# Second dense layer three tiles behind the first, first MoE products in two groups, and a new instruction order

## The chip, the core and the metric

The kernel runs on one core of a Trainium2 chip. The engines are TensorE (PE in the profile; PEld is its weight load), VectorE (DVE), ScalarE (ACT), GpSimd (POOL) and SyncE (SP), which here only issues DMAs. The metric is the device time of one execution in microseconds (us); the median of three runs is compared.

## What is computed

Three stages follow each other: attention in which a query sees only keys of its own hash bucket, a dense mixture of four experts, and a dense block with SoLU and layer norm. The sizes are 2 batches x 768 rows = 1536 tokens, 8 heads of 64, width 512, hidden width 1024.

```python
# attention, per batch and head (768 x 64)
mask = bucket(q @ proj)[:, None] == bucket(k @ proj)[None, :]   # 6 sign bits each
attn = softmax(where(mask, q @ k.T / 8, -1e9)); x = attn @ v
# MoE: every token through all 4 experts
out = sum(p[:, e] * (relu(x @ w1[e]) @ w2[e]) for e in range(4))
# dense block
h = out @ w_in; solu = h * softmax(h)
ln = (solu - mean) / sqrt(var + 1e-6) * g_ln
return ln @ w_out
```

All results have float32 accuracy. The kernel gets it by splitting each operand into a high and a low half (in the 32-bit format that TensorE takes at full rate, or in f16) and adding three products: high x high, high x low, low x high.

## The kernel before

**Staging.** The 12 tiles of 128 tokens form 4 chunks of three. Attention of the first chunk (`attn_first`) runs alone; attention of chunks 1 to 3 is spread over the MoE of chunks 0 to 2; then comes the dense block (`dense`) over all 12 tiles.

**The first chunk's attention.** Keys and queries of the first two heads (`ln` and `y` serve as their buffers) are split, turned by TensorE, projected with `lhs_w` for the sign bits; the other six heads go in pairs (`project_pairs`). For head h, `unit(h)` issues the DMAs that bring operands of its scores from on-chip tiles into two alternating buffers: `kC` (here named wsa_104), `qC` (wsb_106), `kB` and `qB`. Even heads use kB_125 and qB_127, odd heads kB_126 and qB_128. Scores of 128 queries are four matmuls (wsa x wsb and kB x qB, twice); DVE takes the row maximum, ACT the exponential into a `p` tile, TensorE turns p in six 128x128 transposes (`idn,p`), ACT or DVE copies them out, and 6 or 12 matmuls with v follow (`t,hl` for the first four heads, `t,vs` or `xh,vs` later). `av_out` divides, and after every second head splits the result into one quarter (one of KD = 4 slices of 128) of `xh` and `xl`, the operands of the MoE's first products. Between these stand the loads of v for a maximum (`ln<-in_v_dram`, twice 768 KB), of the domain probabilities (`dp`), and of the first expert weights (`wra`, `wrb`).

**The MoE.** `moe_a(c, s)` makes hidden slice s of chunk c: 12 matmuls over the four quarters of xh and xl into one PSUM bank. `split_h` evicts it with ACT (relu, high half) and DVE (low half). `moe_b` multiplies by w2. Weights are split into halves on ACT, POOL and DVE (`wsa`, `wsb` from `wra`, `wrb`).

**The dense block.** `first(i)` makes tile i's hidden row block (24 matmuls of 512 columns in four groups), then a chain of small steps on DVE and ACT (`ln_tiles`), then the high and low halves in f16 (`copy_by`, `sub_by`) and two DMA transposes. `second(i)` makes 24 matmuls of 512 columns in eight groups from them. Program order is first(i), then second(i - lag).

**What sets the order.** Every operation is recorded with its dependencies (`Recorder`), a matmul group as one operation. `emit` then issues them in the order of the table `ORDER`: each number is the place, among the operations still left, of the next one. `FORMS` names the engine of each operation that several can do (A is ACT, V is DVE, G is POOL), `BANKS` its PSUM bank. Each engine works through its own queue in that order. All operations are issued from line 389, so the profile shows that line for all; the tiles tell them apart.

## Time and profile before

| | us |
|---|---|
| median of three runs | 850.31 |
| the three runs | 849.22, 853.28, 850.31 |
| the profiled execution | 850.63 |
| its span, from the first to the last instruction | 848.8 |
| TensorE busy within the span | 827.0 |
| VectorE busy | 673.3 |
| ScalarE busy | 456.1 |
| GpSimd busy | 262.6 |

The span leaves out 1.8 us of the profiled execution. A timeline row gives start, duration, engine, operation and how many were merged; in brackets stands the idle time of the engine ahead of it and what ended it. A matmul's duration has its way through the array in it, so successive ones overlap: three matmuls of 512 columns show 0.81 us and six show 1.46.

### The profile page before, as it was taken

To read this page: it belongs to the slowest core of one execution; us is meant where nothing else is said; L and a number is where in the kernel's file an instruction comes from. 1 tells how busy PE (TensorE), PEld (TensorE's weight loads), DVE (VectorE), ACT (ScalarE), POOL (GpSimd) and SP (SyncE) were. 2 spreads that over 40 slices of the span, in tenths; PEclk is the share of its full clock that TensorE was granted. 3 is DMA by queue.
4 is the path that set the end of the run, shared out by engine and by line. 5 is a ranking of instruction groups with operands and counts; after the bars stand their busy time and mean duration, and the time that the engine had idled before them with its cause. 6 is when DMAs were issued, how large, how long until landed. Compare 5 with 4: busy or idle time off the path is not lost.

```text
span 848.8 us, 13127 instructions
## 1 busy us (share of the span) xinstructions
PE 827.0 (97%) x4431; PEld 529.4 (62%) x4431; DVE 673.3 (79%) x1425; ACT 456.1 (54%) x846; POOL 262.6 (31%) x296
## 2 busy tenths in 40 slices
PE   6898999999999999999999999999999999999998
PEld 5666898888988555656555555555555554444443
DVE  7779868788878999988577898853477989998782
ACT  5658747797874476674325566432145444444331
POOL 2125543466732132343213214241033332210130
PEclk9999999999999999999999999999999999999999
DMA  8787776999999999999756999825249766245352
GB/s 204 204 222 193 203 251 160 264 254 265 271 261 298 293 281 263 266 224 226 165 156 171 245 231 244 215 63 125 75 131 231 258 212 197 79 108 119 81 105 93
DMA packets 241747, 167.83 MB, mean 198 GB/s; under 512 B 167824, under 2 KB 213008, under 8 KB 241680
## 3 DMA queue, kind: packets, MB, share of 16 engines
q1 hardware_dynamic: 241680, 167.00, 75.6%
q8 instruction: 35, 0.57, 0.3%
q14 instruction: 32, 0.26, 0.1%
HBM read 103.51 MB, written 19.73 MB: 145 GB/s over the span
## 4 chain that ended last, share of the span: by engine, by line
PE 79%; DVE 9%; DMA 4%; issue 3%; POOL 3%; ACT 1%; SPq 1%; DVEq 0%; POOLq 0%; ACTq 0%
PE PS L389 79%; DVE ln L389 3%; POOL ln L389 1%; DMA wsb<-wsb 1%; DVE sm L389 1%; SPq L389 1%; DMA ln<-in_moe_w_out_dram 1%; DMA winD<-ln 1%; DMA kD<-stk 1%; DVE tmp L389 1%; DMA ln<-in_moe_w_in_dram 1%; POOL p L389 1%; DVE wsa1h L389 0%; DVE p L389 0%; DMA ln<-in_k_dram 0%
## 5 line engine op out<-in xcount | busy, mean ns | idle before, releaser
L389 ACT ACTIVATE p<-PS,sm 128x768 f32<-128x768 f32 x96 | 95.0, 990 | 39.5 <-POOL sm L389 18.2
L389 DVE TENSOR_REDUCE sm<-PS 128x1 f32<-128x768 f32 x96 | 90.9, 950 | 15.0 <-PE PS L389 13.8
L389 POOL TENSOR_SCALAR sm<-sm 128x1 f32<-128x1 f32 x93 | 33.8, 364 | 152.2 <-DVE sm L389 102.0
L389 PE MATMUL PS<-xh,wsa 128*128 128x384 f32 x256 | 69.7, 337 | 0.0
L389 PE MATMUL PS<-kB,qB 80*128 80x384 f32 x192 | 65.2, 339 | 0.5 <-DMA kB<-vs 0.5
L389 PEld LDWEIGHTS <-hha0h 128*128 128x128 f16 x400 | 37.4, 98 | 40.7 <-issue 3.7
L389 ACT ACTIVATE hha0h<-PS 128x384 f16<-128x384 f32 (+1 forms) x66 | 31.8, 487 | 56.2 <-PE PS L389 56.0
L389 POOL TENSOR_SCALAR ln<-ln 128x512 int32<-128x512 int32 x26 | 36.1, 1388 | 82.1 <-DVE ln L389 69.9
L389 PEld LDWEIGHTS <-wsa1h 128*128 128x128 f16 x408 | 39.6, 98 | 28.7 <-issue 0.6
L389 PE MATMUL PS<-kC,qC 128*128 128x384 f32 x144 | 56.3, 391 | 1.3 <-DVE hxa L389 1.3
L389 PEld LDWEIGHTS <-wsa0h 128*128 128x128 f16 x408 | 39.3, 98 | 28.4 <-issue 1.1
L389 DVE SCALAR_TENSOR_TENSOR hl<-p,sm,hl 128x768 f16<-128x768 f32 x48 | 49.7, 1039 | 8.6 <-POOL hl L389 4.7
L389 PE MATMUL PS<-xh1h,ln 128*128 128x384 f16 x192 | 50.5, 327 | 0.0
L389 DVE SCALAR_TENSOR_TENSOR hxa0h<-PS,hha0h 128x384 f16<-128x384 f32 x64 | 35.0, 550 | 19.2 <-ACT hha0h L389 19.1
L389 PE MATMUL PS<-wsb0h,hha0h 128*128 128x512 f16 x164 | 48.9, 380 | 0.2 <-DVE fit L389 0.2
L389 PEld LDWEIGHTS PS<-xh,wsa 128*128 128x128 f32 x256 | 46.7, 188 | 0.5
L389 PEld LDWEIGHTS <-ln 128*128 128x128 f16 x336 | 32.1, 98 | 22.9 <-issue 1.3
L389 PE MATMUL PS<-wsb1h,hha0h 128*128 128x512 f16 x152 | 45.3, 380 | 0.0
L389 PE MATMUL PS<-xl,wsa 128*128 128x384 f32 x128 | 42.9, 335 | 0.0
L389 PE MATMUL PS<-xh1h,wsa0h 128*128 128x384 f16 x160 | 42.4, 327 | 0.0
L389 PE MATMUL PS<-xh1h,wsa1h 128*128 128x384 f16 x160 | 42.0, 326 | 0.0
L389 PE MATMUL PS<-wsb,hha 128*128 128x512 f32 x132 | 41.9, 398 | 0.0
(331 smaller groups left out, 2262.6 us busy)
## 6 DMA issues: line engine op xcount, KB each, us to landing
wra<-in_moe_w_dram SPq DMA_DIRECT2D x52, 512.0 KB, 5.0
wrb<-in_moe_w_dram SPq DMA_DIRECT2D x52, 512.0 KB, 5.0
kC<-kD SPq DMA_DIRECT2D x24, 384.0 KB, 4.5
kB<-kD SPq DMA_DIRECT2D x24, 240.0 KB, 4.2
vr<-in_v_dram SPq DMA_DIRECT2D x28, 192.0 KB, 4.0
qD<-stk SPq DMA_DIRECT2D x27, 192.0 KB, 3.4
qC<-qD SPq DMA_DIRECT2D x24, 192.0 KB, 3.9
ln<-in_moe_w_in_dram SPq DMA_DIRECT2D x8, 512.0 KB, 4.4
```

The source lines that it names most:

```text
L389: fn(**{key: self.now(x) for key, x in kw.items()})
```

## The change

The program gets the same matmuls, 4399 of them with the same columns in total, and the same 573 DMA issues and branches on SP. Three things differ.

In `moe_a` the first three hidden slices of chunk 0 are recorded as two groups: nine matmuls over the first three quarters, and three over the last. In `dense` the lag is 3. The f16 halves of a tile and their transposes no longer share one of three tiles: the transposes go round four half tiles, the halves alternate between two (both in the tile t320h).

```diff
-        with rec.group():
-            for kk in range(KD):
-                for w, x in ((wh, xh), (wh, xl), (wl, xh)):
+        for part in (range(0, KD - 1), range(KD - 1, KD)) if c == 0 and s < 3 else (range(KD),):
+            with rec.group():
+                for kk in part:
+                    for w, x in ((wh, xh), (wh, xl), (wl, xh)):
...
+        halves = [t.rearrange("p a r q -> p (a r q)")[:, j * 2 * FF2:(j + 1) * 2 * FF2] for t in t16_r.t for j in range(2)]
...
-                x = t16_r.t[i % 3].rearrange("p a r q -> p (a r q)")
-                x16, y16 = x[:, 0:2 * FF2], x[:, 2 * FF2:4 * FF2].rearrange("p (a k q) -> p a k q", a=2, q=128)
+                x16 = halves[4 + i % 2]
+                y16 = halves[i % 4].rearrange("p (a k q) -> p a k q", a=2, q=128)
...
-        lag = 2
+        lag = 3
```

The tables `ORDER`, `FORMS` and `BANKS` are new throughout; of `FORMS` the first line:

```diff
-AVAAVVAVVVAAAAVAAAVAAVVAVAAAAGVAVAVGVAGVAVAVAVAAVGGGAAVAGVAVGAVAVGGVGVGVAGVVVVAAVGVGVVVAGVVAVVAGAAVAVGGVAGAGV
+VGAVAAVAVAAVAAVVAVAAAAVAVAAAVAGVAGGAVVGVGAAVGAVAAVVGAAVAAVVVGAAVVVAVAAAVVVGAGVGGAGGAAAVVAVVAVAAVVGVVVGGVAAAGAG
```

They move operations between engines: DVE has 1369 instructions for 1409, ACT 689 for 686, POOL 338 for 301.

On SP, at the place where the operands of head 2 are sent for (wsa_104 from wsa_105, wsb_106, kB_125, qB_127), the order before was:

```order
L389 DMA wsa_104<-wsa_105 64x768 x2
L389 DMA qB_127<-wsb_106 64x384
L389 DMA dp<-in_moe_domain_probs_dram 128x2x24
L389 DMA kB_125<-wsa_105 64x768
L389 DMA ln_113<-in_v_dram 128x4x384
L389 DMA kB_125<-vs_76 16x768
L389 DMA wsb_106<-wsb_106 64x384 x2
L389 DMA qB_127<-kC_68 16x384
```

The same place now, from the first operand of head 2 on:

```order
L389 DMA wsa_104<-wsa_105 64x768
L389 DMA kB_125<-wsa_105 64x768
L389 DMA ln_113<-in_v_dram 128x4x384
L389 DMA wsb_106<-wsb_106 64x384
L389 DMA wsa_104<-wsa_105 64x768
L389 DMA qB_127<-wsb_106 64x384
L389 DMA vr_73<-in_v_dram 128x384
L389 DMA kB_125<-vs_76 16x768
L389 DMA wsb_106<-wsb_106 64x384
L389 DMA qB_127<-kC_68 16x384
L389 DMA ln_113<-in_v_dram 128x4x384
```

The load of `dp` has left (it now stands among the operands of heads 4 and 5), the first 768 KB load, which stood ahead of the place before, is now third, and the second comes behind the last operand of head 2.

On PE, before the first MoE product (xh_93 x wsa_104), the order before was this, with `t_84,vs_75` the last head's product with v:

```order
L389 MATMUL PS<-idn,p_79 128x128 x6
L389 MATMUL PS<-idr,hl_65 128x128 x3
L389 MATMUL PS<-idr,hl_64 128x128 x3
L389 MATMUL PS<-t_84,vs_75 128x384 x12
L389 MATMUL PS<-stk_67,lhs_w 128x384
L389 MATMUL PS<-idr,hl_65 128x128 x3
L389 MATMUL PS<-idr,hl_64 128x128 x3
L389 MATMUL PS<-stk_66,lhs_w 128x384
L389 MATMUL PS<-stk_67,lhs_w 128x384
L389 MATMUL PS<-stk_66,lhs_w 128x384
L389 MATMUL PS<-xh_93,wsa_104 128x384
```

Now two of the nine-matmul groups begin ahead of head 6's product with v (`xh_94,vs_74`); their end and what follows reads:

```order
L389 MATMUL PS<-xl_95,wsa_104 128x384
L389 MATMUL PS<-xh_93,wsa_104 128x384 x2
L389 MATMUL PS<-xl_95,wsa_104 128x384
L389 MATMUL PS<-xh_93,wsa_104 128x384
L389 MATMUL PS<-idn,p_77 128x128 x2
L389 MATMUL PS<-idn,p_78 128x128 x4
L389 MATMUL PS<-idn,p_77 128x128 x4
L389 MATMUL PS<-xh_94,vs_74 128x384 x4
L389 MATMUL PS<-hha_108,vs_74 128x384 x2
```

So 18 matmuls of the MoE moved ahead of the last two heads' products; the third group of nine stands right behind the last head's.

On POOL, at the end of the dense block, the order before was this; TENSOR_TENSOR with ln_113 makes a tile's low half, TENSOR_SCALAR from ln_113 its high half:

```order
L389 TENSOR_TENSOR t_82<-ln_113,t_82 128x1024
L389 TENSOR_SCALAR wsb1h<-wrb_103,fit 128x1024
L389 TENSOR_TENSOR t_82<-ln_113,t_82 128x1024
L389 TENSOR_SCALAR t_83<-ln_113 128x1024
L389 TENSOR_SCALAR t320h<-ln_113 128x1024
L389 TENSOR_TENSOR t320h<-ln_113,t320h 128x1024
L389 TENSOR_SCALAR t_82<-ln_113 128x1024
L389 TENSOR_TENSOR t_83<-ln_113,t_83 128x1024
```

And now:

```order
L389 TENSOR_SCALAR wsb0h<-wrb_102,fit 128x1024
L389 TENSOR_SCALAR hl_81<-y_112,ys 128x512
L389 TENSOR_TENSOR t320h<-ln_113,t320h 128x1024
L389 TENSOR_SCALAR wsb1h<-wrb_103,fit 128x1024
L389 TENSOR_SCALAR wsb0h<-wrb_102,fit 128x1024
L389 TENSOR_TENSOR t320h<-ln_113,t320h 128x1024
L389 TENSOR_SCALAR t320h<-ln_113 128x1024
L389 TENSOR_TENSOR t320h<-ln_113,t320h 128x1024 x3
L389 TENSOR_SCALAR t320h<-ln_113 128x1024
L389 TENSOR_TENSOR t320h<-ln_113,t320h 128x1024 x3
```

POOL makes eight of the eleven low halves in place of four, and two high halves in place of three.

## Rows read from the trace of the kernel before

**Rows 1.** The page: busy time by engine; the chain that ended last.

```profile
PE 827.0 (97%) x4431; PEld 529.4 (62%) x4431; DVE 673.3 (79%) x1425; ACT 456.1 (54%) x846; POOL 262.6 (31%) x296
...
PE 79%; DVE 9%; DMA 4%; issue 3%; POOL 3%; ACT 1%; SPq 1%; DVEq 0%; POOLq 0%; ACTq 0%
```

**Rows 2.** Stretches: length, busy PE, PEld, DVE, ACT, POOL, granted clock, DMA, GB/s.

```profile
33.00:60.00 27.00, 26.39 (x130) 20.29 (x131) 21.53 (x43) 14.66 (x31) 3.10 (x11) 0.94 0.77 201
60.00:80.00 20.00, 16.22 (x93) 13.27 (x92) 17.88 (x39) 15.56 (x39) 9.87 (x18) 1.00 0.79 198
80.00:95.00 15.00, 13.25 (x85) 11.10 (x84) 13.34 (x33) 12.90 (x30) 11.20 (x16) 1.00 0.59 159
...
300.00:636.00 336.00, 336.00 (x1860) 193.46 (x1859) 255.27 (x477) 167.97 (x316) 93.41 (x119) 1.00 0.79 192
...
735.00:849.00 114.00, 110.02 (x514) 50.24 (x512) 85.33 (x312) 41.59 (x63) 13.88 (x9) 1.00 0.42 95
```

**Rows 3.** Timeline of PE around the first scores of head 2.

```profile
33.08 0.66 PE L389 MATMUL PS<-wsa,wsb 128*128 128x384 f32 x1 [2.26 <-DMA wsb<-wsb]
...
36.43 0.43 PE L389 MATMUL PS<-wsa,wsb 128*128 128x384 f32 x1
```

**Rows 4.** Timeline of SP, the issues between head 0's and head 2's scores.

```profile
20.92 1.11 SPq L389 DMA_DIRECT2D wsa<-wsa  x2
...
22.71 1.35 SPq L389 DMA_DIRECT2D dp<-in_moe_domain_probs_dram  x1
...
25.12 0.59 SPq L389 DMA_DIRECT2D ln<-in_v_dram  x1
...
28.37 0.56 SPq L389 DMA_DIRECT2D qB<-kC  x1
```

**Rows 5.** The chain of waits from 0 to 76 us: start, us, what.

```profile
26.38 6.28 DMA wsb<-wsb
```

**Rows 6.** The start: SP's third issue, and DVE's wait for the key load.

```profile
1.64 1.88 SPq L389 DMA_DIRECT2D ln<-in_k_dram  x3
...
5.08 0.36 DVE L389 CAST t<-ln 128x384 fp32r<-128x384 f32 x1 [0.90 <-DMA ln<-in_k_dram]
```

**Rows 7.** Groups by form on DVE and POOL, 0 to 97 us: count, busy, mean ns.

```profile
L389 DVE COPY t<-PS 128x512 f32<-128x512 f32 x5 | 3.4, 685 | 0.2 <-ACT p L389 0.2
...
L389 DVE TENSOR_TENSOR t<-ln,t 128x384 fp32r<-128x384 f32 x2 | 1.1, 559 | 0.7 <-ACT t L389 0.7
...
L389 POOL TENSOR_SCALAR p<-p,sm 128x768 f32<-128x768 f32 x9 | 8.2, 917 | 1.7 <-DVE sm L389 1.5 <-ACT hha L389 0.2
```

**Rows 8.** Timeline of PE, the end of the first chunk's attention.

```profile
82.86 0.63 PE L389 MATMUL PS<-idn,p 128*128 128x128 f32 x4 [0.24 <-DVE xp L389]
83.97 0.88 PE L389 MATMUL PS<-idn,p 128*128 128x128 f32 x6 [0.48 <-POOL p L389]
...
90.76 2.36 PE L389 MATMUL PS<-t,vs 128*128 128x384 f32 x12 [0.55 <-DVE t L389]
```

**Rows 9.** Timelines of POOL, DVE and PE from 143 to 148 us.

```profile
143.99 2.53 POOL L389 TENSOR_TENSOR wsa<-wra,wsa 128x1024 fp32r<-128x1024 f32 x1 [5.09 <-ACT wsa L389]
...
144.20 2.36 DVE L389 TENSOR_SCALAR big<-big 128x2 f32<-128x2 f32 x1
...
147.07 0.45 PE L389 MATMUL PS<-kC,qC 128*128 128x384 f32 x1 [1.27 <-DVE hxa L389]
```

**Rows 10.** The dense block: SP and PE timelines, then DVE's and POOL's low halves.

```profile
743.83 4.12 SPq L389 DMA_TRANSPOSE t<-t  x2
...
750.74 1.46 PE L389 MATMUL PS<-wsb0h,t 128*128 128x512 f16 x6
...
796.71 0.81 PE L389 MATMUL PS<-wsb1h,t 128*128 128x512 f16 x3
...
L389 DVE TENSOR_TENSOR t<-ln,t 128x1024 f16<-128x1024 f32 x5 | 6.1, 1225 | 0.2 <-ACT t L389 0.2
...
L389 POOL TENSOR_TENSOR t<-ln,t 128x1024 f16<-128x1024 f32 x3 | 6.4, 2133 | 57.9 <-ACT t L389 51.5 <-DVE st L389 6.4
```

More of the change, by code (lines that the diff above doesn't have):

```diff
@@ new lines @@
+GGGAGAAAGVAGGAGGVVGAAGAVAGAAAGAGAVGVGVGGVGVGAAGVVVAGAGAAAGGAGVAVAAGVAGAAGGAVAAAAGGGAAVVAVVGVAAAGGAGAVVAVGVVVVA
+GVAAGAAGVAAVVGVGGAAAAGGVAVVGAGVVAVAGVAAAVVGVVAGVGVAAAGVVAVAGGGAVAGGAGAGVGGAGAVVGVVAGVGVAAVAGGAAGGAAVAGGGVGAAAV
+GGAGGAGAAAVVAGVVGAVVAAVGGGVVAGAVAGVVVVAGVGAAGAGAAGGAGAAAVAAAVVGAAGVAVAAGGGAAVVGVAVVGVAGVGAVAVGVAVAVAVVVGAAGAAV
+AGAVVVAVAVAVVAGAGVAAVAVVVGAVAVGGGVGVVAGGGAAGAVAGAAGAVGAVAAGAVAAAAVVAVAAAAVVGAGGGAGAAAGAGAGGAVAGAAGGAAAGAVAVAVA
+VVGVAAGGAAAVAVGAAVGAAAVAAGAAGAVGAAAGGVAGVVAAAGAGGAAVGVVGVAVVGVAGVAAGVVAGGGVGAGAGVAGGVAAGGVVVGGGGAAGVAAVVGVAAAG
@@ L136 @@
+AVVAGAGGVGGAVAAAGGVGAVVGAVGAGVAGGGVGVVGGAAAVAAVVAGAVAVAAGGGAVAGGVVVAVAVAAVAGGVGAAGGGVGVGVGAGAGGVAGAGGVGAAGAAGG
+VGAVAAAAGGAVGGVAVGGGAGGGAGAAGGVGGGVGGVGGGGVGAAGGAGAAVVVGGVVVVAVGGVVGGGGAVGVGAVGGGGGGVVGGAVVVVGVVVAGVAGVAGVAGAG
+AVAGGAAVGAAAVAVVVAVAAGAVAAVAAAVAAVAVAAGAAVAGAVGGAGAAGGAGGGAGGVVAAVAVAGAVAGVGAGVGAGVGVAAVAVA
 """
 BANKS = """
-13574057136701352170350134163560241306013421602354163571074153102604213601320654315360321560143025406756171076
-10572676573654361205326356357474636353615024362364363634535735436546024613767376766736737637363563467656015725
@@ L141 @@
-76744364634363420163463564763573653164023164653436353436341062341543636743467337447642163045435463461304216436
-45364356633062134614653636436457453012561525763513071236471201203156347625013477346574623105642006436243062146
-054537402
+30653171607534023742503720145641403601342076364201305640206310341643216043061045230413460132453412041276120177
+01273537454641320634365736536535653463140326143246346334634673661430216343676763673636736737363767354567041627
+56764635436341620163456336545643654632051746563436353573756132401361634676437634764701253466434757361026343463
@@ L144 @@
+56343645463052631035743537655316423452072564307350646702153603540314347637204120420640610521642060436243631046
+740246060
 """
@@ L1348, in moe_a @@
         n = 0
-        with rec.group():
-            for kk in range(KD):
-                for w, x in ((wh, xh), (wh, xl), (wl, xh)):
-                    T.matmul(
-                        out=ps[:, 0:N],
-                        lhsT=w[:, kk, j * 128:(j + 1) * 128],
-                        rhs=x[:, kk, 0:N],
-                        start=(n == 0),
-                        stop=(n == 3 * KD - 1),
-                    )
-                    n += 1
+        for part in (range(0, KD - 1), range(KD - 1, KD)) if c == 0 and s < 3 else (range(KD),):
+            with rec.group():
+                for kk in part:
+                    for w, x in ((wh, xh), (wh, xl), (wl, xh)):
+                        T.matmul(
+                            out=ps[:, 0:N],
+                            lhsT=w[:, kk, j * 128:(j + 1) * 128],
+                            rhs=x[:, kk, 0:N],
+                            start=(n == 0),
+                            stop=(n == 3 * KD - 1),
+                        )
+                        n += 1
         hT["m", c, s] = split_h(ps, N, True, c == 0)
```

9 lines of the change are left out of this document (removed), and 200 rows, old and new, of the table ORDER.

## The prediction

> **What bounds the kernel now.** I read the busy times first: TensorE (PE) works 827.0 of the 848.8 us of the span, and the chain that ended last lies on PE for 79% [rows 1]. The stretches then say where the other 22 us lie. From 300 to 636 us PE is busy 336.00 of 336.00 at a granted clock of 1.00, and the dense block is much the same: 110.02 of 114.00, with the last store in it [rows 2]. The change leaves the matmuls and their columns alone, so in the middle there is nothing to win; a new order can only open holes there. The holes that are there lie in the first 100 us, in the first chunk's attention: 16.22 busy of 20.00 from 60 to 80 us and 13.25 of 15.00 from 80 to 95, 5.53 idle together [rows 2].
>
> The causes differ by place. At 33.08 PE has waited 2.26 us for a transfer into wsb, an operand of head 2's scores [rows 3]; from 33 to 60 us the granted clock is 0.94 on average [rows 2], since behind that wait the clock is at the lower of its two levels (1.2 of 2.4 GHz) for a while: the first score matmul takes 0.66 us, where one of the same shape takes 0.43 at 36.43 [rows 3]. From 60 to 95 us DVE is the fullest of the helpers, 17.88 + 13.34 = 31.2 of 35 us busy [rows 2], and PE's brackets name DVE and POOL [rows 8].
>
> The sum goes against the profiled execution, 850.63 us, of which 848.8 is the span and 1.8 lies outside; I leave the 1.8 as it is. The median of the runs, 850.31, is 0.3 below it, so I use one scale for both.
>
> **The change part by part.**
>
> *A, the start.* SP's third row issues three key loads in 1.88 us, 0.63 each, and DVE then waits 0.90 us for the load of head 1's keys [rows 6]. In the new order that load is second and no longer third, up to 0.63 sooner, and the cast would start that much sooner. Against it, one low half of these first keys goes from DVE to POOL. No row has this shape on POOL; in the dense block the same kind costs 2133 ns there against 1225 on DVE [rows 10], a factor of 1.74, so the 559 ns of DVE [rows 7] would become 0.97, 0.41 more. Range -0.9 (the whole wait) to +0.41; I take **-0.5**, nearer to the issue, since other low halves stay on DVE.
>
> *B, head 2's operands.* The chain shows the transfer into wsb from 26.38 us on, 6.28 us long [rows 5], though it is a small on-chip copy. Ahead of it stand two loads of v, 768 KB each; the second was issued at 25.12 [rows 4]. At the 201 GB/s of the stretch behind it [rows 2] one such load is 786,432 bytes / 201 = 3.9 us of the DMA engines. SP itself takes from 20.92 to 28.93 (28.37 + 0.56) for this list, 8.0 us without a pause, 1.35 of them for dp [rows 4]. The new order takes dp out and puts the second 768 KB load behind the last operand; ten issues are left which at about 0.6 us make some 6.4 us, 1.6 sooner. A DMA queue 3.9 us shorter and an issue 1.6 us sooner are against a wait of 2.26, so the wait should go, and with it the half clock, 27.00 x 0.06 = 1.62 us. Together 3.88 at most. The first big load still stands third in the list, and the queries' copies behind it; I take **-3.0**, range -3.88 to 0.
>
> *C, relief of DVE.* Up to the first MoE eviction DVE has eight instructions fewer by the order: four evictions of 128x512 (685 ns each, 2.74 us) and four smaller ones net, each between 0 and 0.559 [rows 7], so 2.7 to 5.0 us. POOL gets rid of four of its nine p<-p,sm at 917 ns, 3.7 us [rows 7]; ACT takes over part of both, and has room: 15.56 of 20 and 12.90 of 15 [rows 2]. What of it reaches PE is bounded by PE's idle time there, 5.53 less D's 1.27, so 4.26. DVE is full to 31.2 of 35, so part of the relief only lengthens its own pauses. I take about half the bound, **-2.0**, range -4.26 to 0. The price if ACT becomes late is the rival of the moved wait, below.
>
> *D, groups of nine.* The three bubbles before 82.86, 83.97 and 90.76 make 0.24 + 0.48 + 0.55 = 1.27 us [rows 8]. Two groups of nine now stand ahead of head 6's product with v. Twelve matmuls of 384 columns take 2.36 us [rows 8], so the 18 bring 3.5 us of work for a time in which PE waits for p to be copied. The third group of nine stands behind the last head's product and covers the way of that head's last quarter into xh. The quarter-wise split of xh and xl was there already, so the groups need no new operand. But only bubbles behind the point where they stand can be filled; I take **-0.8**, range -1.27 to 0.
>
> *E, POOL and DVE side by side.* At 143.99 a POOL instruction of two inputs takes 2.53 us, and at 144.20 a DVE instruction on 128x2 elements takes 2.36 [rows 9]; the two end together (146.52 and 146.56). PE then waits 1.27 for what DVE does next [rows 9]. So one can hold the other up. POOL has 37 instructions more, among them nine more with two inputs of 768 or 1024 elements (30 before). One of the 30 cost PE 1.27. By that rate the nine cost 0.4, and I take **+0.5**. Ends: the place at 147 us goes in the new order, -1.27, or three of the nine fall as badly, +3.8.
>
> *F, the dense block.* A product of 512 columns costs (1.46 - 0.81) / 3 = 0.217 us [rows 10]. The lag is counted in program order; the table decides where the products stand. Between the end of a tile's first layer and its first second-layer product stand, by the order, 133 products before and 124 now for tile 0, 1 to 4 within 9 of before, 122 and 200 for tile 10, 176 and 95 for tile 11; behind the last tile's first layer, up to that tile's own turning by PE, 162 and 72. So the room for tile 0 shrinks by 9 x 0.217 = 1.95 us. In the trace its transposes are issued until 747.95 (743.83 + 4.12) and its first product starts at 750.74 [rows 10]: 2.79 us for the landing, and PE loses nothing. How much of it is slack, no row says. The new t16 halves free the buffers sooner and DVE has fewer steps ahead. For the last tile 72 x 0.217 = 15.6 us are left for its chain. Low halves on POOL are 2133 - 1225 = 0.91 us later [rows 10]. Where the products cover, all of this is free; I take **+0.2**, range 0 to 1.95.
>
> Sum: -0.5 - 3.0 - 2.0 - 0.8 + 0.5 + 0.2 = -5.6, so 850.6 - 5.6 = **845.0 us**. The spread of these terms among themselves is some 2 us either way, 842 to 846 in the likelier half, as B is the largest and can lose little above its value.
>
> **The rivals.**
>
> *The wait moves (848.5).* dp's issue of 1.35 us [rows 4] now stands among the operands of heads 4 and 5, and SP has no pause there to swallow it. For: SP issued the shown list back to back, and each list of operands is as long as the last. Against: by then PE has more heads in work. In this case A and B bring nothing on balance, as another wait with its stretch of half clock stands in the place of the one at 33.08: 850.6 - 2.0 (C) - 0.8 (D) + 0.7 (E, F) = 848.5.
>
> *The lag brings nothing and costs (848).* Tile 0's 2.79 us prove to be the landing alone, so 1.95 us of room are 1.95 us of wait, and one low half on POOL is 0.91 late: 845.0 + 1.95 + 0.91 = 847.9. For: a DMA transpose pair took 4.12 us to issue [rows 10]. Against: the sum over the other tiles is about even.
>
> *POOL holds DVE up (slower, 855.5).* 37 instructions at POOL's mean of 262.6 / 296 = 0.89 us [rows 1] are 33 us more of POOL. If DVE is shut out for a third of it and PE waits for that, 11 us come on top: 845.0 - 0.5 (E is in it) + 11 = 855.5. It decides from 10 us, 30% of the added time. For: the pair at 144 us, where 2.36 of DVE brought 1.27 of wait [rows 9], a half. Against: all 262.6 us of POOL that are there cost PE one such wait, and at 336.00 of 336.00 [rows 2] POOL and DVE were both at work with no loss on PE.
> The Trainium skill ("SBUF — State Buffer", section "Who interferes with whom") says that DVE, in some of its modes or with two operands in SBUF, shares a port pair with GpSimd and that the pair is locked for one of them at a time. The row at 144.20 agrees (2.36 us for 128x2 elements). By that rule alone every long pair would collide and the time would be that of this rival.
>
> *All first-stage terms reach their ends (841).* A -0.9, B -3.88, C -4.26, D -1.27, E and F at +0.7: -0.9 - 3.88 - 4.26 - 1.27 + 0.7 = -9.6, so 841. For: the idle time is there. Against: all ends at once.
>
> **How the numbers follow.** Forecast (842 to 846) 0.46; the wait moves 0.22; the lag costs 0.10; POOL holds DVE up 0.12; all ends 0.10. The range from 839.5 to 852 holds all but the POOL rival and some strays on both sides, about 8 in 10; the low end is about the case of all ends with E at its own lower end (841.0 - 0.5 - 1.27 = 839.2). About 0.5% is what a measurement of this kernel can tell from no change: 846.06 and 854.56. Faster: 0.46 + 0.10, less the forecast's own upper edge, 0.53. Within: 0.22 + 0.10 and that edge, 0.35. Slower: 0.12.
>
> **What would show it.** B: PE's row at head 2's first score has no bracket for wsb, and the granted clock from 33 to 60 us is 1.00; else dp or the first big load wasn't the cause. A: DVE's wait for keys is below 0.90. C: PE's busy time from 60 to 95 us rises per matmul, and DVE's falls below 31.2 for the same work. D: the bubbles before the last two heads' products are gone. E: no row of 128x2 on DVE is over 2 us beside POOL and no wait of PE over 1 us stands behind 147. F: no bracket on PE from 735 us to the store, the last tile included. The forecast is wrong if a bracket of over 2 us stands among heads 3 to 7 (the wait moved), if the clock is granted below 1.00 in a stretch where it was 1.00, or if PE waits in the dense block for a transpose.

## The result, and the profile after

The changed kernel took 857.15 us (median of 13 runs, 853.97 to 859.39); the kernel before took 853.28 in the runs beside it (13 runs, 849.22 to 855.70). The ratio is **1.0057, with an interval of 1.0040 to 1.0074**: slower by some 4.9 us (the two medians stand 3.9 apart). The forecast was 845.0, and the time is outside its range.

The profiled execution of after took 853.97 us, the fastest of the 13; its span is 852.2 against 848.8. The page of after, busy time by engine (compare [rows 1]):

```profile
PE 827.0 (97%) x4431; PEld 529.3 (62%) x4431; DVE 666.7 (78%) x1386; ACT 457.3 (54%) x848; POOL 302.0 (35%) x333
```

PE is busy as long as before, DVE 6.6 us less, POOL 39.4 us more. So the 3.4 us of span are new idle time of PE. Where it lies, the stretches tell; the columns are those of [rows 2], and the number behind each busy time is the count of instructions. First after, over the same bounds as the kernel before below it:

```profile
0.00:20.00 20.00, 14.51 (x78) 12.46 (x78) 14.19 (x33) 9.70 (x20) 4.25 (x11) 1.00 0.86 199
20.00:95.00 75.00, 66.10 (x370) 53.56 (x370) 60.70 (x121) 57.78 (x122) 30.44 (x54) 1.00 0.77 201
95.00:300.00 205.00, 202.60 (x1108) 170.14 (x1107) 167.98 (x307) 138.09 (x256) 101.90 (x92) 1.00 0.95 257
300.00:636.00 336.00, 334.77 (x1852) 192.69 (x1851) 248.73 (x459) 163.94 (x315) 116.70 (x142) 1.00 0.79 191
636.00:735.00 99.00, 98.17 (x514) 50.16 (x513) 89.41 (x164) 46.19 (x77) 25.35 (x23) 1.00 0.69 214
```

And the kernel before (300 to 636 us is in [rows 2]):

```profile
0.00:20.00 20.00, 12.76 (x76) 10.99 (x77) 14.87 (x34) 10.15 (x20) 3.71 (x11) 1.00 0.83 209
20.00:95.00 75.00, 65.92 (x355) 51.91 (x354) 62.89 (x128) 53.17 (x119) 27.75 (x51) 0.98 0.76 198
95.00:300.00 205.00, 203.57 (x1116) 172.19 (x1115) 166.82 (x312) 134.58 (x247) 91.43 (x84) 1.00 0.94 258
636.00:735.00 99.00, 98.79 (x520) 50.58 (x519) 88.08 (x168) 48.62 (x83) 32.43 (x23) 1.00 0.67 209
```

The counts of PE are the ones to read, since both kernels issue the same matmuls; as these differ in length and in order, a count is a coarse measure. At 95 us after has done 448 matmuls (78 + 370) and before 431: it is 17 ahead, which at the mean of the next stretch (202.60 / 1108 = 0.18 us) is 3.1 us. Then it falls behind: 8 fewer to 300 us, 8 fewer to 636, 6 fewer to 735; at 735 us it is 5 behind (a dense product takes 0.22), and the rest, 2.3 of the 3.4 us, comes after that. So in this pair of profiles the start won about half of what the forecast's terms A to D had promised, and the MoE and the dense block lost twice that gain. The lead itself is partly a chance of the executions shown: a second profile of the kernel before had done 444 at 95 us, as no half clock fell into its start. Against that one the lead is 4. A second profile of after had done 455 by then, 11 more than the second of before; it is still 5 ahead at 735 us (3929 against 3924) and loses everything in the dense block. So the waits below are in both profiles of after, but how the loss is spread over the stages is not.

**The start.** The wait at 33.08 of [rows 3] is gone, and from 33 to 60 us the granted clock is 1.00. Three stretches of after, to be read against [rows 2]:

```profile
33.00:60.00 27.00, 24.57 (x125) 18.21 (x125) 19.82 (x43) 17.57 (x37) 3.06 (x10) 1.00 0.89 216
60.00:80.00 20.00, 16.58 (x99) 14.08 (x98) 18.69 (x41) 18.20 (x38) 11.90 (x22) 1.00 0.75 199
80.00:95.00 15.00, 13.60 (x92) 12.67 (x91) 11.56 (x24) 11.57 (x27) 9.99 (x14) 1.00 0.48 145
```

But PE now waits one head later. PE's timeline at head 3's first scores in after:

```profile
38.51 0.41 PE L389 MATMUL PS<-wsa,wsb 128*128 128x384 f32 x1 [1.14 <-DMA wsb<-wsb]
39.90 0.45 PE L389 MATMUL PS<-kB,qB 80*128 80x384 f32 x1 [0.98 <-DMA kB<-vs]
```

and the chain of waits of after from 20 to 45 us (start, us, what), which says why the operand was late:

```profile
27.37 8.66 DMA ln<-in_v_dram
...
36.05 0.48 SPq L389
...
36.58 3.28 DMA kB<-vs
```

SP's issue at 36.05 waited until the second 768 KB load, issued at 27.37, had landed 8.66 us later. The issue has nothing to do with that load's data; between the two stand seven other transfers. By the semaphores of the trace each issue on SP signals its landing on one of eight, in turn, and waits for that same one first, so for the landing of the transfer eight before it. Moving the load behind head 2's operands moved the wait to the transfer that stands eight places behind it.

From 60 us on, ACT is late. Two of PE's waits in after, from its timeline:

```profile
61.87 1.23 PE L389 MATMUL PS<-idn,p 128*128 128x128 f32 x6 [0.62 <-ACT p L389]
...
82.15 0.45 PE L389 MATMUL PS<-idr,hl 128*128 128x128 f32 x3 [0.95 <-ACT p L389]
```

From 20 to 96 us nine waits, 4.8 us, carry ACT's p; in before it was three with 1.4, and DVE and POOL had most of the rest behind 34 us ([rows 8] has some of them).

**The MoE and the dense block.** Here and there a POOL instruction of two inputs starts shortly ahead of a DVE instruction on one or two elements, and the two end together. In after PE waits behind three of these pairs; behind others, as those at 814.99 and 828.15 us, where DVE takes 1.34 and 2.12, it doesn't. Timelines of POOL, DVE, ACT and PE in after, around 184 and 190 us:

```profile
183.31 2.39 POOL L389 TENSOR_TENSOR wsa<-wra,wsa 128x1024 fp32r<-128x1024 f32 x1
...
183.69 2.04 DVE L389 TENSOR_SCALAR fit<-big 128x2 int32<-128x2 int32 x1
...
190.07 0.99 ACT L389 ACTIVATE p<-PS,sm 128x768 f32<-128x768 f32 x1
...
191.21 0.45 PE L389 MATMUL PS<-kC,qC 128*128 128x384 f32 x1 [1.49 <-ACT p L389]
```

around 250 us:

```profile
248.09 1.21 DVE L389 TENSOR_TENSOR wsb<-wrb,wsb 128x1024 fp32r<-128x1024 f32 x1
...
248.30 3.21 POOL L389 TENSOR_TENSOR wsb<-wrb,wsb 128x1024 fp32r<-128x1024 f32 x1 [5.21 <-issue]
...
249.22 2.31 DVE L389 TENSOR_SCALAR fit<-fit 128x2 int32<-128x2 int32 x1
...
252.05 0.45 PE L389 MATMUL PS<-idr,hl 128*128 128x128 f32 x3 [0.54 <-DVE hxa L389]
```

and in the dense block:

```profile
746.00 2.13 POOL L389 TENSOR_TENSOR t320h<-ln,t320h 128x1024 f16<-128x1024 f32 x1 [2.21 <-ACT t320h L389]
...
746.25 1.90 DVE L389 TENSOR_TENSOR st<-st,ys 128x1 f32<-128x1 f32 x1
...
748.18 1.20 ACT L389 ACTIVATE ln<-PS,st,ys 128x1024 f32<-128x1024 f32 x1 [2.26 <-DVE st L389]
...
752.20 1.12 ACT L389 ACTIVATE PS<-ln,st 128x1024 f32<-128x1024 f32 x1
...
753.58 1.46 PE L389 MATMUL PS<-wsb0h,t 128*128 128x512 f16 x6 [2.15 <-ACT PS L389]
```

The ends: 185.70 and 185.73, 251.51 and 251.53, 748.13 and 748.15. It is the pattern of [rows 9]. Elsewhere such a DVE instruction takes about 0.15 us. In each case DVE's next steps lead to the release of a PSUM bank for which PE has work: the scores' bank that ACT reads as p at 190.07; in the dense block the banks of tile 2's first layer, which ACT frees at 752.20 + 1.12. PE waits 1.49 + 0.54 + 2.15 = 4.18 us there. A second profile of after has the same three (2.04, 2.31 and 1.90 us on DVE) and the same waits, 1.49 and 2.14 behind the first and the last; the middle one is 0.22. In that profile the wait in the dense block costs more than its length:

```profile
752.41 2.54 PE L389 MATMUL PS<-wsb0h,t 128*128 128x512 f16 x6 [2.14 <-ACT PS L389]
```

The six products take 2.54 us where the row of the first profile above has 1.46, and the granted clock from 754 to 756 us is 0.50; in the first profile it is 1.00 there. The wait at 147 us [rows 9] is gone in after.

Not every short DVE step beside POOL is held. In the kernel before, around 744 us, POOL and then DVE:

```profile
743.41 2.15 POOL L389 TENSOR_TENSOR t<-ln,t 128x1024 f16<-128x1024 f32 x1 [3.55 <-ACT t L389]
...
743.48 0.15 DVE L389 TENSOR_SCALAR st<-st 128x1 f32<-128x1 f32 x1
...
745.09 0.48 DVE L389 SCALAR_TENSOR_TENSOR st<-st 128x1 f32<-128x1 f32 x1
```

The first DVE step runs at its 0.15 us inside POOL's 2.15; the other, with two inputs, ends with POOL (745.57 and 745.56). In the timelines of before and after 77 such TENSOR_SCALAR steps on one element per partition start inside a POOL instruction of two inputs of over 0.8 us, and none takes more than 0.22 us.

### The profile page after: what moved, and what is told of

The parts are those of the page before. It is cut to its first block, busy times and chain, and to the rows that moved or that the text cites. A ratio compares the mean times of both kernels' runs of the same rounds, so it can differ in the third digit from the quotient of the medians.

```text
span 852.2 us, 13145 instructions
## 1 busy us (share of the span) xinstructions
PE 827.0 (97%) x4431; PEld 529.3 (62%) x4431; DVE 666.7 (78%) x1386; ACT 457.3 (54%) x848; POOL 302.0 (35%) x333
## 4 chain that ended last, share of the span: by engine, by line
PE 80%; DVE 7%; DMA 6%; ACT 3%; issue 2%; POOL 1%; SPq 0%; DVEq 0%; ACTq 0%; POOLq 0%
PE PS L389 80%; DMA ln<-in_v_dram 2%; ACT p L389 1%; DVE ln L389 1%; DVE st L389 1%; POOL ln L389 1%; DMA xl0h<-hl 1%; DMA t<-hl 1%; DMA t320h<-hl 1%; DMA kD<-stk 1%; DVE sm L389 1%; DVE mx L389 1%; DMA qD<-stk 0%; DVE hl L389 0%; SPq L389 0%
## 5 line engine op out<-in xcount | busy, mean ns | idle before, releaser
L389 POOL TENSOR_SCALAR sm<-sm 128x1 f32<-128x1 f32 x104 | 40.7, 392 | 140.1 <-DVE sm L389 109.5
L389 PEld LDWEIGHTS <-wsa0h 128*128 128x128 f16 x408 | 39.4, 98 | 28.4 <-issue 0.8
L389 DVE SCALAR_TENSOR_TENSOR hl<-p,sm,hl 128x768 f16<-128x768 f32 x48 | 52.3, 1090 | 5.8 <-POOL hl L389 3.7
L389 POOL TENSOR_SCALAR ln<-ln 128x512 int32<-128x512 int32 x23 | 25.9, 1127 | 74.4 <-DVE ln L389 66.1
L389 PEld LDWEIGHTS <-t 128*128 128x128 f16 x264 | 25.8, 98 | 33.7 <-issue 3.1
```

The source lines that it names most:

```text
L389: fn(**{key: self.now(x) for key, x in kw.items()})
```

## The experiments

The order of the kernel stands in tables of numbers, so each edit is told in the rows of the order that it moves. "Step" is a place in the program's list of operations; step 570 is at about 95 us, step 3260 at about 705.

**1. The changed start alone.**

```diff
 steps 0 to 569: order and engines of after
-steps 570 on: order and engines of after, lag 3
+steps 570 on: order and engines of before, lag 2
```

> The changed kernel's order up to the end of the first chunk's attention (some 94 us, groups of nine included), then the order of the kernel before for everything behind it, with lag 2 and the old f16 buffers. Theory (the change gains at the start and loses in the MoE and in the dense block, each place for itself): PE's gaps up to 94 us are those of the changed kernel, the waits at 191, 252 and 753 us are gone, the span is 848.8 - 3.3 = 845.5 us, ratio to before about 0.996. Rival (what the start gains is given back by the next stage in any case): the span is 848 to 849, ratio 1.000.

Measured: 1.0042 (1.0022 to 1.0063), 854.97 us. The waits of 191, 252 and 753 us are gone and from 735 us on PE is full, yet the kernel is slower than before. In the profile a new wait stands right behind the seam, on PE:

```profile
103.67 0.73 PE L389 MATMUL PS<-wsb,hha 128*128 128x512 f32 x2 [1.94 <-DVE hxb L389]
```

and the granted clock from 100 to 120 us is 0.91. So the start's gain isn't kept by the old order behind it, and the old order's wait of 1.27 behind the pair of [rows 9] is back (149.14). That what the start hands over (which buffers are filled, what DVE still owes) makes the wait at the seam is likely and not shown. The forecast of a faster kernel fell. The seam has a wait of its own, so this run doesn't price the start by itself.

**2. The old dense block.**

```diff
 steps 0 to 3259: order and engines of after
-steps 3260 on: order and engines of after, lag 3
+steps 3260 on: order and engines of before, lag 2
```

> The changed kernel's order up to some 705 us, then the dense block of the kernel before (its order, lag 2, its f16 buffers). Theory (the dense part costs 3.4 us by itself: a wait of 2.15 us for a PSUM bank at 753.6, 0.8 at 732 and 0.2 at 803): no wait in the dense block, span 852.2 - 3.4 = 848.8 us. Rival (the dense block only collects lateness that the MoE hands on): the wait stays in some form, span 851 to 852.

Measured: 1.0061 (1.0041 to 1.0081), 856.16 us, no better than after. The single wait of 2.15 at 753 gave way to four smaller ones at 715.68 (0.90), 732.27 (0.67), 738.55 (0.94) and 757.04 (0.81). That is nearer to the rival, that the dense block collects what comes late from ahead. What lag and dense order cost by themselves isn't settled by it.

**3. The three POOL low halves left out.**

```diff
 for each step i:
+    if i in (1030, 1388, 3406): continue
     issue step i
```

> The changed kernel without three GpSimd instructions of two inputs: the low half of one wsa block (183.3 us), of one wsb block (248.3 us) and of the first tile of the dense block (746.0 us) are not made, so those low halves hold old data. Nothing else moves. Theory of the held-up DVE (a long GpSimd instruction of two inputs keeps a DVE instruction of two elements from ending: 2.04 us at 183.7, 2.31 at 249.2, 1.90 at 746.3): these three take 0.15 to 0.2 us, the waits of PE at 191.2 (1.49), 252.05 (0.54) and 753.6 (2.15) shrink by 1.5, 0.5 and about 1.7, span 852.2 - 3.7 = 848.5 us. Rival (a lag of three holds too many PSUM banks, so the second layer waits anyway): 191 and 252 go, 753.6 stays at 2 us, span 850.2. Rival (ACT is late for other reasons): the waits stay, 852.

Measured: 0.9988 (0.9966 to 1.0009), 850.47 us, 0.7% below after. DVE's timeline at the first and the second place (with the added lines all operations are issued from line 391):

```profile
186.17 0.16 DVE L391 TENSOR_SCALAR fit<-big 128x2 int32<-128x2 int32 x1
...
250.91 0.15 DVE L391 TENSOR_SCALAR fit<-fit 128x2 int32<-128x2 int32 x1
```

0.16 and 0.15 in place of 2.04 and 2.31, no wait of PE behind them, and at 753.88 PE waits 0.66 for ACT's PS in place of 2.15. By the ratios, three instructions of POOL, 2.39 + 3.21 + 2.13 us long, were worth some 6 us. The waits of PE behind 96 us in the two profiles differ by less, 6.9 in after and 4.2 here. It bears the theory, but with their work gone altogether; what they cost when the work is done elsewhere is asked in experiment 8.

**4. The second load of v late, in after.**

```diff
 L389 DMA wsb_106<-wsb_106 64x384
 L389 DMA qB_127<-kC_68 16x384
-L389 DMA ln_113<-in_v_dram 128x4x384
 L389 DMA qB_128<-kC_68 16x384
```

The load stands at about 73 us now and the seven steps that read it at about 90.

> The changed kernel with the second 768 KB load of v, and the seven small steps that make the scale of v from it, moved from 27 us to 74 us and from 38 us to 90 us; the scale is first used at 101 us. Theory (SP's kB issue at 36.05 waits until that load has landed, as an issue must wait for the eighth issue ahead of it; the waits of PE at 38.5 and 39.9, 1.14 and 0.98 us, come from there): SP has no pause of 1.3 us at 34.8, both waits go, span 852.2 - 2.1 = 850.1 us. Rival (the operands of head 3 are late because of SP's issue time): the waits shrink by under 1 us, span 851.5 or more.

Measured: 1.0055 (1.0038 to 1.0072), 855.31 us. Head 3's two waits are gone. The timelines of PE and DVE from 80 to 96 us show what came instead:

```profile
80.38 0.45 PE L389 MATMUL PS<-idr,hl 128*128 128x128 f32 x3 [1.50 <-ACT p L389]
...
91.14 3.92 PE L389 MATMUL PS<-t,vs 128*128 128x384 f32 x12 [1.06 <-DVE t L389]
...
89.01 1.74 DVE L389 TENSOR_REDUCE vm<-ln 128x1 f32<-128x1536 f32 x1
```

The second of these is a group of twelve that took 2.36 us in [rows 8]; the clock granted from 80 to 100 us is 0.91. The 2.1 us won at head 3 were given back 45 us later, but not by the stage alone: the DVE row is one of the seven moved steps, and it now stands between the steps that make the t for which PE waits. So the run priced the load's move together with this new place of its reader, and doesn't show what the move alone would have been worth.

**5 and 6. Both kernels again.** No edit.

> The kernel before once more, for a second profile of it. If its waits belong to its order, those at 33.1 (2.26 us, wsb), 72.5 (1.68) and 147.1 (1.27) are there again within 0.2 us, and GpSimd again holds the DVE instruction at 144.2 for 2.36 us; span 848 to 850. If they are chance of one execution, some are gone. Whether the clock falls to its lower level after the wait at 33.1 is left open.

> The changed kernel once more. If its waits belong to its order, those at 38.5 and 39.9 (2.1 us together), 191.2 (1.49), 252.05 (0.54) and 753.6 (2.15) are there again; ratio to before 1.004 to 1.0075, span 851.5 to 855. If chance of one execution made them, the MoE and the dense block show other waits.

Measured: before in one run 851.17 us; after 1.0069 (1.0042 to 1.0097), 856.24 us. Before's wait behind the pair of [rows 9] is 1.27 again, at 144.78. The wait for wsb is 1.29 in place of 2.26, without half clock behind it; with the same start it is 2.10 in the profile of 9 and 0.61 in that of 11. So a part of what term B wanted to win isn't in each execution.

**7. ACT's new work back on POOL.**

```diff
-L389 ACT ACTIVATE p_78<-p_78,sm_90 128x768
-L389 ACT ACTIVATE p_79<-p_79,sm_91 128x768
-L389 ACT ACTIVATE p_77<-p_77,sm_87 128x768
-L389 ACT ACTIVATE wsa_104<-wra_100 128x1024
+L389 POOL TENSOR_SCALAR p_78<-p_78,sm_90 128x768
+L389 POOL TENSOR_SCALAR p_79<-p_79,sm_91 128x768
+L389 POOL TENSOR_SCALAR p_77<-p_77,sm_87 128x768
+L389 POOL TENSOR_SCALAR wsa_104<-wra_100 128x1024
```

> The changed kernel with four instructions of the first chunk's attention back on GpSimd, as in the kernel before, that the change put on ACT: three p<-p,sm (at 60.9, 62.5 and 70.9 us, 0.93 each) and one wsa<-wra (80.1 us, 1.05). Theory (ACT became the bound of the stretch from 55 to 75 us, 17.2 of 20 us busy for 13.5 before): PE's waits at 61.9, 63.5, 64.6 and 82.2 us (0.62, 0.39, 0.45, 0.95, all for ACT p) go down by 1.0 to 2.0 together, span 851, ratio 0.998 to 1.000 of the changed kernel. Rival (DVE and GpSimd bound the stretch just as much): the waits take POOL's or DVE's name, their sum stays within 0.5 us.

Measured: 1.0105 (1.0082 to 1.0128), 858.71 us, the slowest of all, though its interval overlaps that of after in the same set of runs (1.0042 to 1.0097). PE at 64 us:

```profile
63.94 0.66 PE L389 MATMUL PS<-idn,p 128*128 128x128 f32 x4 [1.27 <-POOL p L389]
```

The waits only changed the name of who is late: from 60 to 90 us they sum to 4.1 us here and to 4.2 in after. What this profile has more is half clock behind them (0.83 from 60 to 80 us). The theory that ACT's added work alone made the start slow fell; that POOL would do it worse isn't settled.

**8. The three low halves on DVE.**

```diff
-L389 POOL TENSOR_TENSOR wsa_104<-wra_100,wsa_104 128x1024
-L389 POOL TENSOR_TENSOR wsb_107<-wrb_103,wsb_107 128x1024
-L389 POOL TENSOR_TENSOR t320h<-ln_113,t320h 128x1024
+L389 DVE TENSOR_TENSOR wsa_104<-wra_100,wsa_104 128x1024
+L389 DVE TENSOR_TENSOR wsb_107<-wrb_103,wsb_107 128x1024
+L389 DVE TENSOR_TENSOR t320h<-ln_113,t320h 128x1024
```

On DVE each stands behind the short step that it had held up (wsb_107 also behind hxa).

> The changed kernel with the same three GpSimd instructions of two inputs (at 183.3, 248.3 and 746.0 us) made on DVE, each behind the DVE instruction that was late or that PE needs. Theory of the held-up DVE: DVE does each in about 1.2 us and nothing is held for 2 us; the waits at 191.2 and 252.05 fall to under 0.3 each, the one at 753.6 (2.15) by 0.5 to 1.5, span 849 to 850.5, ratio to before 1.000 to 1.003. Rival (DVE is full there, and what it takes over costs what the holding cost): the waits stay, ratio 1.0055.

Measured: 1.0028 (1.0015 to 1.0040), 852.74 us. Beside after's 1.0069 in the same set of runs that is 0.4%, some 3.5 us, back. The waits of 191 and 252 are gone; that of 753 fell to 1.15, where the low half now takes its time on DVE itself. Two others are longer than in the profile of after, at 222.87 (1.18, for ACT's p) and 733.51 (1.23, ACT's t320h); both come in other runs with after's order at these places too (1.72 and 1.18 at the first in 2 and 4, 1.22 at the second in 4 and 11), so they aren't this edit's. So the pairs are a cause, and not the only one: without them the changed order is still not faster than before.

**9. The same in the kernel before.**

```diff
 L389 DVE SCALAR_TENSOR_TENSOR hxb_111<-PS,hhb_109 128x384
+L389 DVE TENSOR_TENSOR wsa_104<-wra_100,wsa_104 128x1024
 L389 DVE TENSOR_REDUCE sm_89<-PS 128x1
 ...
 L389 POOL TENSOR_SCALAR sm_88<-sm_88 128x1
-L389 POOL TENSOR_TENSOR wsa_104<-wra_100,wsa_104 128x1024
 L389 POOL TENSOR_SCALAR sm_89<-sm_89 128x1
```

> The kernel before with one instruction moved: the low half of one wsa block, on GpSimd at 143.99 us (2.53), is made on DVE, behind the two hxa and hxb steps that PE needs. Theory of the held-up DVE: the instruction at 144.2 takes 0.15 instead of 2.36, PE's wait at 147.07 (1.27) goes, nothing else changes: span about 847.6, ratio 0.9985 (near what a comparison can tell). Rival (DVE loses as much by the added 1.2 us): the wait stays over 0.8 us.

Measured: **0.9981 (0.9962 to 1.0000), 849.71 us**, the lowest ratio of all, and just at the edge of what can be told from no change. DVE from 144 to 147 us, to be read against [rows 9]:

```profile
144.27 0.16 DVE L389 TENSOR_SCALAR big<-big 128x2 f32<-128x2 f32 x1
...
145.28 1.22 DVE L389 TENSOR_TENSOR wsa<-wra,wsa 128x1024 fp32r<-128x1024 f32 x1
```

The same work takes DVE 0.16 + 1.22 in place of the 2.36 that it was held up alone, and POOL nothing in place of 2.53. PE's stretch from 140 to 160 us, first in before and then here:

```profile
140.00:160.00 20.00, 18.73 (x96) 16.58 (x95) 16.05 (x28) 17.35 (x31) 5.33 (x6) 1.00 0.89 215
```

```profile
140.00:160.00 20.00, 20.00 (x105) 17.59 (x105) 16.39 (x33) 17.35 (x31) 4.11 (x6) 1.00 1.02 245
```

One instruction moved, 1.27 us of wait gone in the profile, and 0.19% of the time (1.6 us), which an interval up to 1.0000 doesn't show by itself. Beside after's 1.0057 this is some 0.8%.

**10. The forecast's term B, done alone in before.** dp with its three steps later, and the second 768 KB load behind head 2's last operand, its readers where they were.

```diff
-L389 DMA dp<-in_moe_domain_probs_dram 128x2x24
 L389 DMA kB_125<-wsa_105 64x768
-L389 DMA ln_113<-in_v_dram 128x4x384
 L389 DMA kB_125<-vs_76 16x768
 L389 DMA wsb_106<-wsb_106 64x384 x2
 L389 DMA qB_127<-kC_68 16x384
+L389 DMA ln_113<-in_v_dram 128x4x384
 ...
 L389 DMA wsb_106<-qC_70 64x384
+L389 DMA dp<-in_moe_domain_probs_dram 128x2x24
 L389 DMA wsa_104<-wsb_107 64x768
```

> The kernel before with one part of the change alone: the load of dp (and the three small steps on it) goes to where the change has it, among the operands of head 5, and the second 768 KB load of v goes behind the last operand of head 2. My prediction's term B: the wait of 2.26 us at 33.1 goes, with the half clock behind it where there is one; span 845 to 847, ratio 0.996 to 0.998. Theory that the wait only moves on: a wait of 1 to 2 us for wsb or kB stands at the first scores of head 3 (SP held until the second load has landed), and what is left of the gain is under 1 us: ratio 0.999 to 1.001.

Measured: 1.0054 (1.0030 to 1.0077), 856.71 us. The wait for wsb is gone, as B said. PE's next wait in this kernel (0.81 more follows at 37.68), and the stretch behind it:

```profile
36.60 0.27 PE L389 MATMUL PS<-idn,big 128*1 128x128 f32 x1 [2.43 <-DVE t L389]
```

```profile
40.00:60.00 20.00, 19.84 (x83) 15.04 (x81) 12.60 (x24) 8.50 (x17) 2.34 (x8) 0.81 0.68 178
```

The steps that read the load (they make v's scale, and PE takes part with two tiny matmuls) now wait for it, with all that stands behind them in order, and the half clock follows: 20 x 0.19 = 3.8 us. Moving a load without its readers made a wait into a larger one.

**11. The changed MoE and dense block behind the old start.**

```diff
-steps 0 to 569: order and engines of after
+steps 0 to 569: order and engines of before
 steps 570 on: order and engines of after, lag 3
```

> The counterpart of the run with the new start alone: the order of the kernel before up to the end of the first chunk's attention (some 97 us), then the changed kernel's. Theory (what the change costs lies in the MoE and in the dense block: 1.5 and 0.5 us at 191 and 252 and some 2 us more up to 335, then 2 to 4 us around 753): these waits are there, the start is that of before; span 852.5 to 855.5, ratio 1.004 to 1.008, the ratio of the changed kernel or more. Rival (the new start is what costs): ratio within 0.002 of 1.

Measured: 1.0061 (1.0042 to 1.0079), 856.80 us, the same as the whole change. PE in the MoE and the dense block of this kernel:

```profile
191.86 0.44 PE L389 MATMUL PS<-kC,qC 128*128 128x384 f32 x1 [1.49 <-ACT p L389]
...
753.59 1.45 PE L389 MATMUL PS<-wsb0h,t 128*128 128x512 f16 x6 [1.84 <-ACT PS L389]
```

The same waits at the same places. So the loss lies behind 95 us. It is also the plainest measure of the new start: with the old one in its place the changed kernel takes 1.0061, with the new one 1.0057 (and 1.0069 in 6), so the new start is worth nothing that can be measured.

**12. 9 and 10 together.** Both diffs as above.

> The kernel before with both of the edits to it: the low half at 144 us on DVE, dp and the second load of v later. If both theories hold, the wait at 147 is gone and at most half of the gain at head 2 is kept: span 845 to 847, ratio 0.996 to 0.998, a kernel faster than both. If head 2's wait only moves, ratio 0.998 to 0.9995.

Measured: 1.0040 (1.0022 to 1.0058), 855.13 us. As 10 (2.72 at 37.25, granted clock 0.82 from 40 to 60 us), with the wait of 147 us gone as in 9: the two add.

**13. 9, and the load with its readers late.** In before: the edit of 9, dp late, the second load at 75 us, its nine steps from 85 to 105 us.

```diff
-L389 MATMUL PS<-idn,big 1x128
-L389 MATMUL PS<-vm,one 128x1
 ...
 L389 MATMUL PS<-t_84,vs_75 128x384 x12
+L389 MATMUL PS<-idn,big 1x128
 ...
 L389 MATMUL PS<-xh_93,wsa_104 128x384
+L389 MATMUL PS<-vm,one 128x1
```

> The kernel before with term B done in full: dp and its three steps later, the second 768 KB load of v at 75 us, and the nine small steps that make scales from it moved along to 85 to 105 us (in the earlier run they stayed, and PE waited 2.43 us for them at 36.6); the low half at 144 us on DVE as before. Term B as forecast: no wait for operands of heads 2 and 3, nothing in its place, span 848.8 - 1.3 (144 us) - 3 = 844.5, ratio 0.994 to 0.996. Theory that the first stage gives it back (DVE and ACT are busy nine tenths from 55 to 95 us and have to do the same work): the waits from 55 to 95 us grow by 1.5 to 3 us, span 846 to 847.5, ratio 0.997 to 0.999, no better than the run with the low half alone (0.998).

Measured: 1.0010 (0.9987 to 1.0032), 851.59 us, no better than 9 alone. From 20 to 60 us no wait of PE is over 0.8 us and the clock is 1.00. Then, PE and DVE:

```profile
88.66 2.35 PE L389 MATMUL PS<-t,vs 128*128 128x384 f32 x12 [2.14 <-DVE t L389]
...
86.26 1.74 DVE L389 TENSOR_REDUCE vm<-ln 128x1 f32<-128x1536 f32 x1
```

In before the same group waits 0.55 [rows 8]; the 1.59 more are again the moved reduction of 1.74 us, which now stands between the steps that make this t. The other long wait of the stretch (1.66 at 68.85, for DVE's sm) isn't new: before has it with 1.68, at 72.53. So, as in 4, what the operands' waits give is taken back before 95 us, and what takes it here is the edit's own step; that the stage would take it back in any case is not shown.

**14. dp alone, in before.**

```diff
-L389 DMA dp<-in_moe_domain_probs_dram 128x2x24
 L389 DMA kB_125<-wsa_105 64x768
 ...
 L389 DMA wsb_106<-qC_70 64x384
+L389 DMA dp<-in_moe_domain_probs_dram 128x2x24
 L389 DMA wsa_104<-wsb_107 64x768
```

> The kernel before with the load of dp (1.35 us of SP) and its three steps alone moved to where the change has them; both loads of v stay. If dp's issue was what made head 2 late, the wait at 33.1 shrinks by about 1.35 us and the half clock behind it may go: span 846 to 848, ratio 0.997 to 0.999. If the two loads of v are (the eighth issue behind each waits until it has landed), the wait stays within 0.5 us: ratio 0.999 to 1.001.

Measured: 1.0026 (1.0011 to 1.0041), 853.48 us. PE:

```profile
32.17 0.66 PE L389 MATMUL PS<-wsa,wsb 128*128 128x384 f32 x1 [2.18 <-DMA wsb<-wsb]
...
62.65 0.59 PE L389 MATMUL PS<-kB,qB 80*128 80x384 f32 x1 [2.05 <-DMA kB<-vs]
```

The wait at head 2 stays at 2.18 (2.26 before). The operand was sent for 1.65 us sooner (24.73 against 26.38), and its transfer took longer, 7.13 us against the 6.28 of [rows 5], so in this profile dp's place on SP didn't decide when it landed. As this wait lies between 0.61 and 2.26 in four profiles of one order, one profile can't rule out a part for dp. Where dp now stands, among head 5's operands, a wait of 2.05 is new. That is the place and the mechanism of the rival "the wait moves"; but in 10, 12 and 13, where dp stands among the same operands, this wait is 0.76 to 0.90, and 0.49 in before, so 2.05 is the most that one execution showed.

## Why the prediction was wrong

Two steps failed. The terms of the start, A to D, were to bring 6.3 us, each bounded by the wait that it removes; by experiment 11 they brought nothing that can be measured. And E, put at +0.5 from a rate of losses per POOL instruction, came out at +2.9 in PE's waits and at some 3.5 to 6 us in the runs that took its three pairs away. Its size decided that the kernel got slower.

**A, the start (-0.5).** The wait for head 1's keys has gone, as it said. The new low half on POOL took 1.00 us, where 0.97 had been worked out. What was missed is who waits: PE's first product. Timelines of POOL and PE in after:

```profile
3.61 1.00 POOL L389 TENSOR_TENSOR t<-ln,t 128x384 fp32r<-128x384 f32 x1 [2.32 <-DVE t L389]
...
4.66 1.76 PE L389 MATMUL PS<-idr,t 128*128 128x128 f32 x12 [4.66 <-POOL t L389]
```

PE starts at 4.66, in before at 4.24. It makes that up by 20 us in this pair of profiles (14.51 busy against 12.76), hardly in the other (13.20 against 13.02), so how right the size was isn't settled.

**B, head 2's operands (-3.0).** The wait at 33.08 and its half clock went; by 10 and 14, with one profile each, it was the load's move that took it away rather than dp's. Yet the gain was not kept. First, the load's move put a wait of 1.14 + 0.98 at head 3, since SP's issue eight places on waits for its landing; the step had taken SP's list as a sum of issue times and missed that an issue can wait for an earlier landing. Second, moving the load further, with its readers (4 and 13), took away the operands' waits and gave nothing that can be measured, but there the moved reduction itself held up the last head's product; what the stage would have kept without that stays open. The step bounded the gain by the wait that it removed and left out the load's readers and the transfer eight places on. (Its ten issues at about 0.6 us are 6.0 and not 6.4, which changes nothing.) The half clock is no fixed part of it either: it was behind the wait in one profile of before (0.94 from 33 to 60 us) and not in the other.

**C (-2.0) and D (-0.8).** DVE's busy time from 60 to 95 us fell from 31.2 to 30.2, with 191 matmuls of PE in place of 178, and the bubbles behind POOL's p and DVE's t are mostly gone; in their place stand the waits for ACT's p, 4.8 us from 20 to 96. Of A to D together, -6.3 in the sum, 3.1 us can be seen at 95 us, and 0.7 us (4 matmuls by 0.18) against the other profile of before. By experiment 11 it is nothing. It is the rival "the wait moves" in part. Step C had put ACT's lateness at nothing because ACT had room, 15.56 of 20 us from 60 to 80; it is now busy for 18.20 of them. But its added work alone isn't the cause, since giving four of its steps back to POOL (7) left the sum of the waits as it was; that ACT's place in the chain from scores to p is, is argued and not shown.

**E, POOL and DVE side by side (+0.5).** This is the term that failed most. The mechanism was named, with its row; the size came from a rate, one loss in 30 instructions. Such a rate says nothing here, because what a pair costs is decided by what DVE has next: three of the added ones met a short DVE step on a chain that frees a PSUM bank, and cost PE 4.18 us (0.66 of it stayed when the three were left out), of which the wait at 147 that went gives 1.27 back. +2.9 net was inside the step's range and not near its value. Left out, the three were worth some 6 us (3), put on DVE some 3.5 (8); that this is more than the waits fits the half clock that follows the wait at 752 in the second profile, though no run isolates it. The rival "POOL holds DVE up" had the cause, but its 11 us, a third of all added POOL time, was too much by half or more.
The Trainium skill ("SBUF — State Buffer", section "Who interferes with whom") has a rule for this that the rows bear out: a DVE instruction with two inputs in SBUF, or a tensor_scalar in a two-port mode, and a POOL instruction that reads SBUF lock each other out, and the one that was issued first goes first. Of the held instructions two are tensor_scalar and one has two inputs. At 248.09 it is DVE that is first, for 1.21 us: POOL's instruction then takes 3.21, 1.00 of it beside DVE's rest, and holds the next one of DVE for 2.31. That the whole added time of POOL comes back as waits, as the prediction took the rule by itself to mean, the rows don't show: the short steps on one element at 743.48 and elsewhere aren't held, and from 300 to 636 us POOL is busy 116.70 us against 93.41 [rows 2], 23.3 more, and PE loses 1.23.

**F, the dense block (+0.2).** The place was right, tile 0's first second-layer product; the mechanism wasn't. Not the landing of its transposes is late but a PSUM bank: tile 0's product is given a bank of tile 2, and waits until ACT is done with it. This isn't the lag's doing: in the order of both kernels the first layers of tiles 0 to 5 stand ahead of this product, and in both it gets the same bank. What differs is how late the bank comes free. In before ACT's last step on it is

```profile
747.44 1.12 ACT L389 ACTIVATE PS<-ln,st 128x1024 f32<-128x1024 f32 x1 [1.94 <-DVE st L389]
```

and in after the one at 752.20. From the end of tile 2's first layer to the release it took 13.2 us before (735.4 to 748.6) and 17.4 now (735.9 to 753.3), of which 1.75 are the pair at 746; the rest lies in the order of DVE's and ACT's steps ahead of tile 2's exponential, and no run isolates it. The step counted products between two places on PE and left out whose bank the product needs. What stays of the wait without the pair is 0.66 in 3 and 1.15 in 8, where DVE is busier.

**The end of the sum.** The start -3.1 (or -0.7), E and F and smaller waits for ACT behind 95 us +6.4: +3.3 in the profile, +4.9 by the ratio. Of the 6.4 the three pairs explain 4.18 less 1.27; the wait at 732.26 for ACT's t320h is 0.83; four small ones (0.37 at 293.70 for a DMA, 0.82 and 0.41 at 318.54 and 333.06 for ACT's p, 0.24 at 803.19) are 1.8, against 0.3 of such waits in before, and no run isolates their cause. The 1.2 left are in no wait; the count of matmuls isn't exact to that.

**What stays open:** the price of the lag alone; what the load's move is worth with its readers out of the way; why the half clock comes in some executions and not in others of the same program; whether the changed start would be worth something with a MoE order made for it.

## What to carry to other kernels

Before work moves from DVE to POOL, list at each of its places which DVE instruction comes within its two or three microseconds and who waits for that: a two-input instruction on POOL can cost DVE nearly its whole length there (1.9 to 2.4 us here), and moving just one such (9) did better than the whole new order. In every run here that took a wait out of the first stage another came up before its end, twice through the edit's own moved step, so cost the stage by its last wait and not by the wait removed. When a load is moved in a queue, look at its readers and at the transfer eight places behind it too.
